# Stretches of 26 and 22 fill products, and written step orders, in a fused attention and token-MLP kernel

## The chip, the cores and the metric

One Trainium2 chip; the program runs on one of its cores. Its engines are TensorE (PE, with its weight loads shown apart as PEld), VectorE (DVE), ScalarE (ACT), GpSimd (POOL) and SyncE (SP, which issues the DMAs). The metric is the time of one execution in device microseconds; lower is better. A profile is one execution of the program as the hardware profiler saw it, and its times count from the first instruction.

## The reference

The input x has 2048 tokens of 640 channels. Two branches are computed from it and mixed by a gate per token.

```
g = sigmoid((x * gate_w).sum(-1, keepdims=True))
q = (x @ wq) in 32 heads of 20;  k = x @ wk;  v = x @ wv       # one k and one v of 20 for all heads
a = softmax(q k^T * 20**-0.5) v, heads side by side, @ wo
h = layernorm(x)                                                # per token
b = (gelu(h^T @ w1 + b1) @ w2 + b2)^T                           # over the tokens: 2048 -> 1728 -> 2048, per channel
out = g * a + (1 - g) * b
```

## The kernel before

Everything heavy is a matmul on TensorE, and the kernel uses the array in two halves of 64 rows. The contraction of a score (20 numbers, in a split of high and low parts, 60 or 62 rows) and that of an MLP product (64 rows at a time) each fill one half, so that two matmuls run side by side. A half is called a lane here.

**The steps.** Four kinds of work go to TensorE in the main loop:

- *F*, a fill product: one 64-row part of the MLP or of the output projection, 320 columns wide. In the first MLP product it stands at line 1069, in the second at 866, in the output projection at 1005. All fill products of one result add up in one PSUM bank, `g_bank`.
- *s*, a score tile (line 677): 128 keys by 512 queries into a PSUM bank of its own. ScalarE takes its exponential into a tile `p` (line 686), and the bank is free again.
- *m*, a tile for the row maxima of a later group of queries (line 508): 128 queries by 512 keys into a PSUM bank. VectorE reduces it to a maximum (line 514), and the bank is free again.
- *PV*, the product of the exponentials with v (line 788): all 128 rows of the array at once, into a bank that ScalarE copies to `part` (line 800) and GpSimd adds to a running sum (line 801).

Seven banks (three `ms`, three `s`, one `o`) go round among *s*, *m* and PV. `bank_take` and `bank_give` (475 to 484) decide while the program is written which bank a step gets: the one that a small clock of the planner expects to be free first. On the chip semaphores hold the step until that bank really is free.

**The loop.** It has 244 stretches, then a tail. In a stretch one lane (the X lane) runs scores and maxima, the other (the F lane) fill products and one or two *m* or *s*. Both lanes end in a PV of two key blocks; then the lanes change roles. Stretches 0 to 83 carry the first MLP product, 84 to 211 the second, 212 to 243 the output projection. The stretch numbers count from 0; stretch 0 stands ahead of the first PV.

One result of the first MLP product takes 96 fill products, 48 in each lane. `batches` (1078) cuts each lane's 48 into two, at 24, so that a result takes four stretches of 24. Of its 16 token blocks each has three fill products: high weights by high inputs, high weights by low inputs, low weights by high inputs. The weights come in quarters of four token blocks, that is 12 fill products in a lane: a DMA brings `wr`, GpSimd casts it to `wh` (133) and subtracts to `wl` (134). Per result the four quarters are called for by `w1_upto` at the ends of stretches of the result before.

**The order in a stretch.** `main` (1163) has for each length of a stretch a pattern: one string for the X lane, one for the F lane around its fill products.

```
    PATTERN = {24: ("msmsmmssmsmmsmss", "Fm"), 20: ("smsmssmmsmmssm", "mFs"), 21: ("smsmsmmssmmsmsm", "Fs"),
               15: ("smsmssmsmss", "mFs")}
```

So a stretch of 24 has 16 steps in the X lane and, in the F lane, 24 fill products and an *m*: 17 steps that take a bank, beside PV. How the two lanes are woven into the one instruction stream is a rule: at each turn the lane comes next that is free first by the planner's clock (an *s* or *m* takes 0.232 us there, an *F* 0.147 us), with a bank's expected release counted in for *s* and *m*. The lengths 20 and 21 belong to the second MLP product, 15 to the output projection.

Of the kernel before, what the change touches and what calls it, by code (L numbers as in the profile page):

```python
# [18 lines left out]
S, D, H, DH, F = 2048, 640, 32, 20, 1728  # L19
# [11 lines left out]
TAIL = 24  # L31
BLOCKS = (2, 3, 3, 4, 4, 4, 4)
NA = 8
SIXES = range(3)
LAST_M = 2
M_FIRST = 1
# [8 lines left out]
def mix_kernel(ctx: ExitStack, tc: tile.TileContext, A_x, A_wq, A_wk, A_wv, A_wo,  # L45
# [427 lines left out]
    USE = {"exp": ("act", 0.43, 0.477, 0.65), "max": ("dve", 0.43, 0.6, 0.735), "sum": ("dve", 0.35, 0.47, 0.6)}  # L473

    def bank_take():
        i = min(range(len(pool)), key=lambda j: pool[j][0])
# [193 lines left out]
    def qk(u, pr, b):  # L670
        n, kb = units[u]
        assert n in back_in
        if kb == 4 and pr == 0 and b == 0:
            new_q(n + 1)
        q = qtiles[n]
        s = lead_bank() if ps_l else bank_take()
        nc.tensor.matmul(s, kst[64 * b:64 * b + 62, kb * P:(kb + 1) * P], q[64 * b:64 * b + 62, pr, :],  # L677
                         start=True, stop=True)
        ready[u] = 0.0 if ps_l else max(ready.get(u, 0.0), bank_give(s, "exp"))
        p = next_p()  # L680
        ptiles[u, 2 * pr + b] = p

        behind, last["ins"] = last["ins"], None

        def exp():
            e = nc.scalar.activation(p, s, AF.Exp, scale=SCALE)  # L686
# [88 lines left out]
    otile, sums = [], [None]  # L775
    later = []

    def pv_group(us, keep=False):
        n, kb = units[us[0]]
        assert units[us[-1]][0] == n  # L780
        if not otile:
            otile.append(bank_take())
        o = otile[0]
# [5 lines left out]
                                 start=opened and i == 0, stop=(i == len(us) - 1) and (ends or not keep),  # L789
                                 skip_group_check=True)  # L790
        if not keep:
            begin = max(clock["act"], clock["pv"] + 0.14)
            clock["act"] = begin + 0.477
            pool.append((begin + 0.65, otile.pop()))
            if kb == 0:
                sums[0] = ev.tile([P, NB], F32, name="acc", bufs=2)
                nc.scalar.activation(sums[0], o, AF.Copy)
            else:
                part = ev.tile([P, NB], F32, name="part", bufs=2)
                nc.scalar.activation(part, o, AF.Copy)  # L800
                nc.gpsimd.tensor_add(sums[0], sums[0], part)  # L801
# [276 lines left out]
    def batches(tiles, counts):  # L1078
# [57 lines left out]
    AHEAD, DRAIN, ENTER, FIRST = 4, 0.19, 0.138, 0.1  # L1136
# [3 lines left out]
    def pattern(k):  # L1140
        return PATTERN[len(ph[k][0])]

    base = [[pattern(k)[int(k % 2 != h)].count("m") for k in range(len(ph))] for h in range(2)]

    def share(k):
        left = [32 * NU - x for x in given]
# [7 lines left out]
    lanes = [0.0, 0.0]  # L1154
    fresh = [True, True]

    def issue(b, us, f, t):
        clock["now"] = max(t, clock["now"])
        f()
        lanes[b] = clock["now"] + us + (FIRST if fresh[b] else 0.0)  # L1160
        fresh[b] = False

    def main(k, vs, n_max):
        b = k % 2
        fs, rest, done = ph[k]
        fs, done = list(fs), list(done)
        known, kept = set(row_max), set(sent)
        end = 2 * ((vs[-1] if vs else -1) + 1)
        xs, side = pattern(k)
        before, after = side.split("F")  # L1170
        need = end + AHEAD - sc[b]
        if xs.count("s") < need:
            i = len(xs) * 2 // 3
            xs = xs[:i] + "s" * (need - xs.count("s")) + xs[i:]
        while xs.count("s") > need:
            i = xs.rindex("s")
            xs = xs[:i] + xs[i + 1:]
        if xs.count("m") < n_max[b]:
            xs += "m" * (n_max[b] - xs.count("m"))
        while xs.count("m") > n_max[b]:  # L1180
            i = xs.rindex("m")
            xs = xs[:i] + xs[i + 1:]
        after += "m" * (n_max[1 - b] - (before + after).count("m"))
        while (before + after).count("m") > n_max[1 - b]:
            if "m" in after:
                after = after.replace("m", "", 1)
            else:
                before = before.replace("m", "", 1)
        before = "s" * (end - sc[1 - b] - (before + after).count("s")) + before
        xs, before, after = list(xs), list(before), list(after)  # L1190
        total, count = len(xs) + len(before) + len(after) + len(fs), 0
        while fs or after or before or xs:
            if count == (total + 1) // 2:
                settle()
            count += 1
            free = min(e for e, _ in pool)
            tx = max(lanes[b], free) if xs else 1e9
            tf = 1e9
            if before or (after and not fs):
                tf = max(lanes[1 - b], free)  # L1200
            elif fs:
                tf = lanes[1 - b]
            if len(xs) == 1 and fs and not after:
                tx = 1e9
            if tf < tx or tf == tx and not before:
                if before or not fs:
                    c = (before or after).pop(0)
                    issue(1 - b, X_US, (s_next if c == "s" else ms_next)(1 - b) or (lambda: None), tf)
                else:
                    issue(1 - b, F_US, fs.pop(0), tf)  # L1210
                    while done and not fs:
                        done.pop(0)()
            else:
                c = xs.pop(0)
                issue(b, X_US, (s_next if c == "s" else ms_next)(b) or (lambda: None), tx)
        ms_done()
        spare[0] = len(row_max) == NU
        settle(len(vs) == 2)
        if vs:
            n, kb = units[vs[0]][0] + 1, units[vs[0]][1]  # L1220
            if n in kept and n in qtiles and n not in back_in:
                fetch_max(n)
                back_in.add(n)
        for f in rest:
            f()
        for i in sorted(known - sent):
            store_max(i)
            sent.add(i)
        if vs:
            start = max([max(lanes) + DRAIN, min(e for e, _ in pool)] + [ready[v] for v in vs])  # L1230
            clock["pv"] = start + len(vs) * PV_US + ENTER
            lanes[:] = [clock["pv"]] * 2
            fresh[:] = [True, True]
            pv_group(vs)

    ps_l.clear()
# [6 lines left out]
    v = 0  # L1243
# [165 lines left out]
```

## Time and profile before

| | |
|---|---|
| runs | 1607.21, 1607.86 and 1607.96 us; median 1607.86 us |
| profiled execution, its span from the first to the last instruction | 1606.5 us |
| granted TensorE clock | 1.000 |
| busy: PE, DVE, ACT, POOL | 1600.9, 1355.0, 1309.1, 867.6 us |
| from the first PV (161.75 us) to the end of the first MLP product (656.26 us) | 494.51 us |
| second MLP product, to 1372.30 us | 716.04 us |
| output projection, to 1526.46 us | 154.16 us |
| tail, to 1606.5 us | 80.04 us |

The profiled execution's own time is its span; what the runs' median has beyond it (1.4 us) lies around the program. A PE that is busy all the time is not a PE at its peak here: a matmul counts as busy in one lane while the other lane may stand idle. So the busy shares do not say how much there is to gain, and the reading goes by single stretches: from one PV to the next, what is the last thing that PV waits for?

### The profile page before, as it was taken

To read this page: it belongs to the slowest core of one execution; us is meant where nothing else is said; L and a number is where in the kernel's file an instruction comes from. 1 tells how busy PE (TensorE), PEld (TensorE's weight loads), DVE (VectorE), ACT (ScalarE), POOL (GpSimd) and SP (SyncE) were. 2 spreads that over 40 slices of the span, in tenths; PEclk is the share of its full clock that TensorE was granted. 3 is DMA by queue.
4 is the path that set the end of the run, shared out by engine and by line. 5 is a ranking of instruction groups with operands and counts; after the bars stand their busy time and mean duration, and the time that the engine had idled before them with its cause. 6 is when DMAs were issued, how large, how long until landed. Compare 5 with 4: busy or idle time off the path is not lost.

```text
span 1606.5 us, 39460 instructions
## 1 busy us (share of the span) xinstructions
PE 1600.9 (100%) x14864; PEld 1123.2 (70%) x14864; DVE 1355.0 (84%) x2301; ACT 1309.1 (81%) x2566; POOL 867.6 (54%) x976
## 2 busy tenths in 40 slices
PE   9999999999999999999999999999999999999999
PEld 7899677767776777666666666666666666666676
DVE  6689999999999999888888888888888888766644
ACT  4546888888888888888888888888888888999974
POOL 6568676768777687644544434454544333344420
PEclk9999999999999999999999999999999999999999
DMA  7655223323233323222222122222222112245521
GB/s 218 212 171 143 73 74 80 86 64 94 76 81 85 82 67 80 64 73 81 73 70 68 51 67 67 70 73 81 73 73 69 54 50 68 85 123 181 165 87 57
DMA packets 183750, 145.07 MB, mean 90 GB/s; under 512 B 38291, under 2 KB 145424, under 8 KB 183560
## 3 DMA queue, kind: packets, MB, share of 16 engines
q1 hardware_dynamic: 183272, 142.23, 31.4%
q8 instruction: 117, 1.92, 0.5%
q14 instruction: 73, 0.60, 0.1%
q10 hardware_dynamic: 288, 0.33, 0.1%
HBM read 108.75 MB, written 32.15 MB: 88 GB/s over the span
## 4 chain that ended last, share of the span: by engine, by line
PE 98%; DVE 1%; POOL 0%; ACT 0%; issue 0%; DVEq 0%; POOLq 0%
PE s L788 16%; PE ms L788 11%; PE g L866 11%; PE s L677 10%; PE g L1069 9%; PE ms L677 9%; PE ms L508 6%; PE s L508 6%; PE pp L307 4%; PE o L677 3%; PE o L508 2%; PE g L1005 2%; PE o L788 2%; PE s L720 1%; PE g L720 1%; PE s L960 1%
## 5 line engine op out<-in xcount | busy, mean ns | idle before, releaser
L514 DVE TENSOR_REDUCE mp<-ms 128x1 f32<-128x512 f32 x889 | 583.1, 682 | 79.8 <-PE ms L508 64.9
L686 ACT ACTIVATE p<-s 128x512 f32<-128x512 f32 x938 | 543.2, 617 | 39.6 <-PE ms L788 12.8
L514 DVE TENSOR_REDUCE mp<-s 128x1 f32<-128x512 f32 x759 | 503.2, 683 | 75.1 <-PE s L508 61.0
L686 ACT ACTIVATE p<-ms 128x512 f32<-128x512 f32 x808 | 471.9, 614 | 35.1 <-PE s L788 11.8
L801 POOL TENSOR_TENSOR acc<-acc,part 128x512 f32<-128x512 f32 x213 | 275.0, 1291 | 311.2 <-ACT part L800 300.8
L677 PE MATMUL s<-qst,kst 62*128 62x512 f32 x944 | 362.9, 407 | 0.0
L508 PE MATMUL ms<-kst,qmx 60*128 60x512 f32 x889 | 357.5, 416 | 0.0
L677 PE MATMUL ms<-qst,kst 62*128 62x512 f32 x810 | 319.1, 407 | 0.0
L1069 PE MATMUL g<-slot,wh 64*128 64x320 f32 x1344 | 306.1, 313 | 0.3 <-ACT p L686 0.3
L508 PE MATMUL s<-kst,qmx 60*128 60x512 f32 x759 | 304.0, 414 | 0.2 <-DVE mp L514 0.2
L788 PE MATMUL s<-p,v_sb 128*32 128x512 f32 x2240 | 269.3, 598 | 0.0
L1069 PEld LDWEIGHTS g<-slot,wh 64*128 64x128 f32 x1344 | 216.6, 185 | 70.1 <-issue 49.4
L134 POOL TENSOR_TENSOR wl<-wr,wh 128x512 fp32r<-128x512 f32 (+1 forms) x176 | 218.1, 1239 | 28.0 <-ACT wh L131 16.3
L514 DVE TENSOR_REDUCE mp<-o 128x1 f32<-128x512 f32 x308 | 210.1, 682 | 18.5 <-PE o L508 17.8
L677 PEld LDWEIGHTS s<-qst,kst 62*128 62x128 f32 x944 | 174.2, 185 | 59.1 <-ACT p L686 27.6
L1069 PE MATMUL g<-slot,wl 64*128 64x320 f32 x672 | 205.4, 306 | 0.0
L866 PE MATMUL g<-u,wh 64*128 64x320 f32 x864 | 196.5, 309 | 0.0
L866 PE MATMUL g<-slot,wh 64*128 64x320 f32 x864 | 196.4, 309 | 0.0
L677 PEld LDWEIGHTS ms<-qst,kst 62*128 62x128 f32 x810 | 150.0, 186 | 56.8 <-ACT p L686 28.3
L788 PE MATMUL ms<-p,v_sb 128*32 128x512 f32 x1560 | 189.4, 598 | 0.0
L686 ACT ACTIVATE p<-o 128x512 f32<-128x512 f32 x273 | 168.3, 617 | 12.7 <-PE ms L788 6.9
L508 PEld LDWEIGHTS ms<-kst,qmx 60*128 60x128 f32 x889 | 164.2, 185 | 3.6
(270 smaller groups left out, 3101.8 us busy)
## 6 DMA issues: line engine op xcount, KB each, us to landing
wr<-in_B_w_dram SPq DMA_DIRECT2D x136, 256.0 KB
qmx<-q_scr SPq DMA_DIRECT2D x192, 80.0 KB
qst<-q_scr SPq DMA_DIRECT2D x192, 80.0 KB
ot<-l_scr SPq DMA_DIRECT2D x120, 64.0 KB
y_scr<-yo SPq DMA_DIRECT2D x16, 320.0 KB
slot<-o_scr SPq DMA_DIRECT2D x16, 320.0 KB
o_scr<-ot SPq DMA_DIRECT2D x124, 40.0 KB
o_scr<-acc SPq DMA_DIRECT2D x124, 40.0 KB
```

Of the source, the lines that this page charges most:

```text
L134: nc.gpsimd.tensor_sub(wl[:, :nv], wr[:, :nv], f32(wh[:, :nv]))
L307: nc.tensor.matmul(pp, w, t, start=first and n == 0, stop=not more and n == len(steps) - 1)
L508: nc.tensor.matmul(ms, qmax[n][64 * b:64 * b + 60, pr, qt * P:(qt + 1) * P], kst[64 * b:64 * b + 60, kq * NB:(kq + 1) * NB], start=True, s ...
L514: r = nc.vector.tensor_reduce(mtiles[n][:, c, kq:kq + 1], ms, axis=AX.X, op=ALU.max)
L677: nc.tensor.matmul(s, kst[64 * b:64 * b + 62, kb * P:(kb + 1) * P], q[64 * b:64 * b + 62, pr, :], start=True, stop=True)
L686: e = nc.scalar.activation(p, s, AF.Exp, scale=SCALE)
L720: nc.tensor.matmul(pu[r][:, :HD2], w[rows, c, :], h[rows, st, :], start=(st == 0 and k == 0), stop=(st == NS - 1 and k == 2))
L788: nc.tensor.matmul(o[32 * hh:32 * hh + 32, :], v_sb[:, kb + i, :], ptiles.pop((u, hh)), start=opened and i == 0, stop=(i == len(us) - 1) a ...
L801: nc.gpsimd.tensor_add(sums[0], sums[0], part)
L866: other_tile(half, nc.tensor.matmul(hold["p"][:, :HD2], w[r, i, :], u[d][r, fc, :], start=(hold["n"] == 1), stop=(hold["n"] == 6 * FC - 3)))
L1005: other_tile(half, nc.tensor.matmul(hold["p"][:, :HD2], o[r, c, :], w[r, c, d * HD2:(d + 1) * HD2], start=(hold["n"] == 1), stop=(hold["n" ...
L1069: other_tile(half, nc.tensor.matmul(hold["p"][:, :HD2], w[r, st % HS, :], h[d][r, st, :], start=(hold["n"] == 1), stop=(hold["n"] == 6 * NS)))
```

## The change

A result's 48 fill products of a lane are cut at 26, not at 24: two stretches of 26 fill products, one in each lane, then two of 22. The patterns and the rule that wove the lanes are gone. For each length a string gives the whole order of a stretch, both lanes in one; capital *M* and *S* are steps in the F lane. Where the number of steps does not fit (at the loop's ends), `fit` drops or adds some. The planner's clock, which still picks the banks, has new constants and a new notion of when a step starts (`issue`). A bank whose exponential must wait for the next PV, because all `p` tiles are taken, is kept out of the pool until that PV. In the tail, the blocks of PV from the fourth on call for the scores one step ahead per lane, not two.

```diff
+FIRST_F = 26
...
-    X_US, F_US, PV_US = 0.232, 0.147, 0.858
+    X_US, F_US, PV_US, LOAD = 0.2335, 0.147, 0.858, 0.1
...
+        if not ps_l and len(ptiles) >= len(ring):
+            late.append(pool.pop()[1])
...
+        while late:
+            pool.append((max(clock["now"], clock["act"]) + 2 * PV_US, late.pop()))
...
-                cut = [[len(r) * j // cnt for j in range(cnt + 1)] for r in rows]
+                cut = [[0, first, len(r)] if first else [len(r) * j // cnt for j in range(cnt + 1)] for r in rows]
...
-    seq = batches([b1_jobs(*t) for t in todo], [2] * len(todo))
+    seq = batches([b1_jobs(*t) for t in todo], [2] * len(todo), FIRST_F)
...
-    PATTERN = {24: ("msmsmmssmsmmsmss", "Fm"), 20: ("smsmssmmsmmssm", "mFs"), 21: ("smsmsmmssmmsmsm", "Fs"),
-               15: ("smsmssmsmss", "mFs")}
+    AHEAD, ENTER, EXIT = 4, 0.108, 0.135
+    ORDER = {26: "mFFsFmFsFFsFFmFmFsFFFsFmFFmFFsFFmFFmFFmFsMFs",
+             22: "sFmFFsFFFmsFFFmFssFFmFFFssFFFmmFFFsFmM",
+             20: "MsmFFsFsFsFFFFmFFsmFmFFFFmsFsFFsFFMm",
+             21: "MsFsFFmmFFsFFssFFFmsFFmFFFsmFFmFFsFFm",
+             15: "MsmFFsFFsFFmFsFFsFFmsFFFsFSm"}
...
+    def issue(h, us, f, free=0.0):
+        clock["issue"] = max(clock["issue"] + 0.004, begun[h], free)
+        begun[h] = clock["now"] = max(lanes[h], clock["issue"] + LOAD)
+        lanes[h] = begun[h] + us
+        f()
...
+            if c == "F":
+                issue(1 - b, F_US, fs.pop(0))
...
+                h = b if c in "sm" else 1 - b
+                step = (s_next if c in "sS" else ms_next)(h)
+                if step:
+                    issue(h, X_US, step, min(e for e, _ in pool))
...
-        ends = [min(2 * len(units), 2 * (v + n) + 2) for _ in range(2)]
+        ends = [min(2 * len(units), 2 * (v + n) + (2 if n < 3 else 1)) for _ in range(2)]
```

The changed program has the same matmuls as before, in other places. A stretch of 26 takes nine *m* and eight *s* in the X lane and one *M* in the F lane (18 steps with a bank), one of 22 seven *m*, eight *s* and one *M* (16); 20, 21 and 15 keep their numbers (16, 16 and 13).

The end of stretch 21, a stretch of the first MLP product, on TensorE as it was; `g` is the fill's bank, L677 a score, L508 a maxima tile, L788 the PV:

```order
L1069 MATMUL g<-slot_83,wh 128x320
L677 MATMUL s<-qst,kst 128x512
L1069 MATMUL g<-slot_83,wh 128x320
L1069 MATMUL g<-slot_83,wl 128x320
L508 MATMUL o<-kst,qmx 128x512
L1069 MATMUL g<-slot_83,wh 128x320 x2
L677 MATMUL ms<-qst,kst 128x512
L1069 MATMUL g<-slot_83,wl 128x320
L677 MATMUL ms<-qst,kst 128x512
L508 MATMUL ms<-kst,qmx 128x512
L788 MATMUL s<-p,v_sb 32x512 x8
```

The last maxima tile is the F lane's *m*, and it stands last of all. The same end in the changed program, where stretch 21 has 26 fill products (lines: L1074 fill, L678 score, L509 maxima, L793 PV), with the tiles' numbers:

```order
L509 MATMUL o_2334<-kst_71,qmx_3377 128x512
L1074 MATMUL g_1185<-slot0_83,wh_3955 128x320
L1074 MATMUL g_1185<-slot0_83,wl_3956 128x320
L509 MATMUL s_1186<-kst_71,qmx_3377 128x512
L1074 MATMUL g_1185<-slot0_83,wh_4141 128x320
L678 MATMUL ms_2331<-qst_3238,kst_71 128x512
L509 MATMUL s_1188<-kst_71,qmx_3377 128x512
L1074 MATMUL g_1185<-slot0_83,wh_4141 128x320
L678 MATMUL ms_2333<-qst_3238,kst_71 128x512
L793 MATMUL ms_2332<-p_4203,v_sb_72 32x512
```

The F lane's maxima tile now has a fill product and a score behind it, and the two fill products that came over from the later stretches read `wh_4141`, the cast of the weights' third quarter. Before, that quarter's first reader opened the third stretch of a result (stretch 22), as here:

```order
L1069 MATMUL g_1185<-slot0_83,wh_4141 128x320
L508 MATMUL s_1186<-kst_71,qmx_3367 128x512
L1069 MATMUL g_1185<-slot0_83,wh_4141 128x320
L677 MATMUL ms_2333<-qst_3234,kst_71 128x512
L1069 MATMUL g_1185<-slot0_83,wl_4142 128x320
```

In the changed program its first reader stands near the end of the result's first stretch (stretch 20), where the last three rows before PV are the same kinds of steps as in stretch 21 above.

More of the change, by code (lines that the diff above doesn't have):

```diff
@@ L773, in other_tile @@
         last["half"], last["ins"] = half, ins
-    otile, sums = [], [None]
+    otile, sums, late = [], [None], []
     later = []
@@ L791, in pv_group @@
         if not keep:
-            begin = max(clock["act"], clock["pv"] + 0.14)
+            begin = max(clock["act"], clock["pv"] + 0.336)
             clock["act"] = begin + 0.477
-            pool.append((begin + 0.65, otile.pop()))
+            pool.append((begin + 0.657, otile.pop()))
             if kb == 0:
@@ L1076, in b1_jobs, with batches @@
                         for st in range(NS) for k in range(3)], done)]
-    def batches(tiles, counts):
+    def batches(tiles, counts, first=None):
         out = []
@@ L1135, in mix_kernel, with order @@
     FREE_AT, ACT_AT = (0.3, 0.3, 0.3, 0.6, 1.3, 0.0, 0.3), 0.5
[L1136 to L1143 removed]
+    AHEAD, ENTER, EXIT = 4, 0.108, 0.135
[4 more added lines that the diff above has]
+             15: "MsmFFsFFsFFmFsFFsFFmsFFFsFSm"}
+    def order(k):
+        return ORDER[len(ph[k][0])]
+    base = [[order(k).count("m" if k % 2 == h else "M") for k in range(len(ph))] for h in range(2)]
     def share(k):
@@ L1152, in share, with fit @@
         return [c[k] - (i == h and k % 4 == 1 and k < m and over[h] > 0) for i, c in enumerate(base)]
[L1154 to L1158, printed above, removed]
-        f()
-        lanes[b] = clock["now"] + us + (FIRST if fresh[b] else 0.0)
-        fresh[b] = False
+    lanes, begun = [0.0, 0.0], [0.0, 0.0]
+    clock["issue"] = 0.0
+    def issue(h, us, f, free=0.0):
+        clock["issue"] = max(clock["issue"] + 0.004, begun[h], free)
+        begun[h] = clock["now"] = max(lanes[h], clock["issue"] + LOAD)
+        lanes[h] = begun[h] + us
+        f()
+    def fit(order, c, n):
+        while order.count(c) > n:
+            i = order.rindex(c)
+            order = order[:i] + order[i + 1:]
+        while order.count(c) < n:
+            i = order.rindex("F") * 2 // 3
+            order = order[:i] + c + order[i:]
+        return order
     def main(k, vs, n_max):
@@ L1168, in main @@
         end = 2 * ((vs[-1] if vs else -1) + 1)
[L1169 to L1186, printed above, removed]
-            else:
[L1188 to L1215, printed above, removed]
@@ new lines, in main @@
+        tokens = fit(order(k), "s", end + AHEAD - sc[b])
+        tokens = fit(fit(tokens, "m", n_max[b]), "M", n_max[1 - b])
+        tokens = "S" * (end - sc[1 - b]) + tokens
+        for i, c in enumerate(tokens):
+            if i == (len(tokens) + 1) // 2:
+                settle()
+            if c == "F":
+                issue(1 - b, F_US, fs.pop(0))
+                while done and not fs:
+                    done.pop(0)()
+            else:
+                h = b if c in "sm" else 1 - b
+                step = (s_next if c in "sS" else ms_next)(h)
+                if step:
+                    issue(h, X_US, step, min(e for e, _ in pool))
@@ L1216, in main @@
+        assert not fs and not done
         ms_done()
@@ L1229, in main @@
         if vs:
[L1230 to L1233, printed above, removed]
+            start = max([max(lanes) + ENTER, min(e for e, _ in pool)] + [ready[v] for v in vs])
+            clock["pv"] = start + len(vs) * PV_US
+            clock["issue"] = clock["pv"] + EXIT
+            lanes[:] = begun[:] = [clock["issue"]] * 2
             pv_group(vs)
```

2 lines of the change are left out of this document (1 added, 1 removed).

## The prediction

> **What bounds the kernel now.** The page first, its busy times; its chain of waits, too, runs on TensorE nearly all the way.
>
> ```profile
> PE 1600.9 (100%) x14864; PEld 1123.2 (70%) x14864; DVE 1355.0 (84%) x2301; ACT 1309.1 (81%) x2566; POOL 867.6 (54%) x976
> ```
>
> That hides the idle half of the array. So next come the stages, by the view of stretches of time restricted to the PV line (16 matmul records per PV):
>
> ```profile
> 161.75:656.26 494.51, 159.69 (x1329) 34.76 (x1329) 1.00 0.31 79
> 656.26:1372.30 716.04, 246.26 (x2048) 53.57 (x2048) 1.00 0.24 68
> ```
>
> The first MLP product has 1328/16 = 83 stretches of 494.51/83 = 5.958 us from PV to PV and the second 128 of 5.594. Now one stretch, 21, in the timeline of TensorE:
>
> ```profile
> 280.87 1.93 PE L788 MATMUL s<-p,v_sb 128*32 128x512 f32 x16
> 282.72 0.41 PE L1069 MATMUL g<-slot,wh 64*128 64x320 f32 x1
> 282.73 0.49 PE L508 MATMUL ms<-kst,qmx 60*128 60x512 f32 x1
> 282.97 0.30 PE L1069 MATMUL g<-slot,wh 64*128 64x320 f32 x1
> 283.06 0.39 PE L677 MATMUL ms<-qst,kst 62*128 62x512 f32 x1
> ...
> 285.47 0.45 PE L1069 MATMUL g<-slot,wh 64*128 64x320 f32 x2
> 285.65 0.39 PE L677 MATMUL s<-qst,kst 62*128 62x512 f32 x1
> ...
> 286.20 0.30 PE L1069 MATMUL g<-slot,wl 64*128 64x320 f32 x1
> ...
> 286.39 0.50 PE L508 MATMUL ms<-kst,qmx 60*128 60x512 f32 x1
> 286.82 0.64 PE L788 MATMUL s<-p,v_sb 128*32 128x512 f32 x4
> ```
>
> PV holds the array 282.72 - 280.87 = 1.85 us. Call 282.72 the stretch's zero. Fill products follow each other by (286.20 - 282.97)/22 = 0.147 us, steps of the X lane by (285.65 - 283.06)/11 = 0.235 us. The first of a lane takes 0.10 more: 0.25 to the second fill, 0.33 to the second step. The end:
>
> ```profile
> 286.39 0.18 PEld L508 LDWEIGHTS ms<-kst,qmx 60*128 60x128 f32 x1
> ```
>
> The F lane's last fill at 286.20 left that lane free at 286.35, yet the weights of its *m* load only at 286.39. A load that had to wait costs its lane 0.10 again, as at the start, so this *m* counts from 286.49; PV follows at 286.82, that is 0.235 for the *m* and some 0.095 to change over. The wait costs 286.49 - 286.35 = 0.14 us. What ended it is VectorE:
>
> ```profile
> 283.26 1.29 DVE L514 TENSOR_REDUCE mp<-ms 128x1 f32<-128x512 f32 x2 [0.36 <-PE ms L508]
> ...
> 285.66 0.68 DVE L514 TENSOR_REDUCE mp<-ms 128x1 f32<-128x512 f32 x1
> ```
>
> Two single reductions are left out between these rows, so the last row is the stretch's fifth; it ends at 285.66 + 0.68 = 286.34, and the load follows 0.05 later. VectorE came out of PV idle (0.36) and works without a gap from 0.54 on, a bank every 0.60: at 1.22, 1.82, 2.42, 3.02, 3.62. ScalarE's banks:
>
> ```profile
> 282.92 0.60 ACT L800 ACTIVATE part<-s 128x512 f32<-128x512 f32 x1 [1.17 <-PE s L788]
> 283.55 0.60 ACT L686 ACTIVATE p<-ms 128x512 f32<-128x512 f32 x1
> 284.04 1.22 ACT L686 ACTIVATE p<-s 128x512 f32<-128x512 f32 x2
> 285.16 1.08 ACT L686 ACTIVATE p<-ms 128x512 f32<-128x512 f32 x2
> 286.11 0.62 ACT L686 ACTIVATE p<-s 128x512 f32<-128x512 f32 x1
> ```
>
> The copy frees its bank at 0.80, exponentials at 1.43 and then about every 0.48 where a score is there (the pair at 285.16 takes 1.08, one alone 0.60). Up to 286.34 that is the copy, five exponentials and five reductions: eleven. Six banks were free at zero (seven less PV's); a step beyond the sixth waits for a release, the seventeenth for the eleventh. So **the bound is the seventeenth bank**, not a lane's work.
>
> **The first MLP product, worked out.** A step that gets its bank late can count from the release plus 0.05 plus 0.10.
>
> *26.* F lane: 0.10 + 26 x 0.147 + 0.235 = 4.157. X lane: 0.10 + 17 x 0.235 = 4.095. The order begins as before, *m* then *s*, so VectorE keeps its times. The scores stand earlier (second, fourth, fifth, eighth step), so ScalarE need not pause: 0.80, 1.43, 1.91, 2.39, 2.87, 3.35, 3.83. The eleventh release is still 3.62 and goes to the *M*, which counts from 3.77; its own place, behind 25 fills, is 0.10 + 25 x 0.147 = 3.775. Nothing is lost there. The twelfth, 3.83, goes to the last *s*: it counts from 3.98 against 3.86 and ends at 4.215. Without that wait the end is 4.157. I take 4.19, as ScalarE's clock moves by a few hundredths from stretch to stretch; PV to PV 4.19 + 0.095 + 1.85 = 6.135, between 6.10 and 6.16.
>
> *22.* F lane 0.10 + 22 x 0.147 + 0.235 = 3.57, X lane 0.10 + 15 x 0.235 = 3.625. The order begins with *s*, the first *m* is a step later, so VectorE's times are 0.235 later: 1.455, 2.055, 2.655, 3.255. ScalarE's, from a stretch of the second product that begins with a score (zero 753.55):
>
> ```profile
> 753.73 0.60 ACT L800 ACTIVATE part<-o 128x512 f32<-128x512 f32 x1 [0.30 <-PE o L788]
> 754.23 0.59 ACT L686 ACTIVATE p<-ms 128x512 f32<-128x512 f32 x1
> ...
> 756.13 0.65 ACT L686 ACTIVATE p<-s 128x512 f32<-128x512 f32 x1
> ```
>
> that is 0.78, 1.27 and every 0.48: 1.75, 2.23, 2.71, 3.19. Sixteen steps need the tenth release, 3.255; the last *M* counts from 3.405, ends at 3.64. PV to PV 3.65 + 0.095 + 1.85 = 5.595, between 5.57 (lanes alone) and 5.66 (a release 0.06 later).
>
> Mean (6.135 + 5.595)/2 = 5.865, against 5.958: 0.093 x 84 stretches = **7.8 us less**. The cut by itself gains nothing: the longer lane's mean is (4.157 + 3.625)/2 = 3.891 against 0.10 + 24 x 0.147 + 0.235 = 3.863 before. The gain is the 0.14 of waiting, less this 0.03 and the rests above. Bounds: lanes alone, 3.891 + 1.945 = 5.836, gains 10.2 us; the old 0.14 kept on both, 5.976, loses 1.5 us.
>
> **The rest.** A stretch of 20 keeps its 16 steps. Its end before (same stretch of the second product):
>
> ```profile
> 753.55 0.49 PE L677 MATMUL ms<-qst,kst 62*128 62x512 f32 x1
> 757.26 0.64 PE L788 MATMUL ms<-p,v_sb 128*32 128x512 f32 x4
> ```
> ```profile
> 756.83 0.18 PEld L677 LDWEIGHTS s<-qst,kst 62*128 62x128 f32 x1
> ```
>
> The last score loads 0.05 behind the exponential that ends at 756.78, the tenth release, and PV follows at 756.83 + 0.10 + 0.235 + 0.095. A new order asks for the tenth release too, and ScalarE cannot give it earlier: 0, for 96 stretches. Bounds: lanes alone, 0.10 + 20 x 0.147 + 2 x 0.235 = 3.51, would be 0.10 less each (9.6 us); 0.03 more each for another order's misfits is 2.9 us. A stretch of 21 waits for PV's own bank:
>
> ```profile
> 764.69 0.49 PE L677 MATMUL s<-qst,kst 62*128 62x512 f32 x1
> 768.47 1.92 PE L788 MATMUL ms<-p,v_sb 128*32 128x512 f32 x16
> ```
> ```profile
> 767.81 0.61 ACT L686 ACTIVATE p<-ms 128x512 f32<-128x512 f32 x1
> ```
>
> ScalarE frees it at 768.42, PV starts at 3.78. The new order puts an *M* and an *s* first, so the eleventh release is VectorE's 3.62, and the lanes decide: 0.10 + 15 x 0.235 + 0.095 = 3.72. That is 0 to 0.06 for 32 stretches; half of it is **1.0 us less**. The projection's 15 keep their 13 steps: 0, with 0.02 either way, 0.6 us. The tail's two deferred scores per block change places, not number: 0, within two steps, 0.5 us. Banks held out of the pool, and the new constants, only choose which bank; that is in the bounds.
>
> Sum: -7.8 - 1.0 = -8.8; I take 0.6 off for misfits of an order that cannot give way (below). Against the profiled 1606.5 that is 1598.3, against the runs' median 1607.86 - 8.2 = **1599.7 us**.
>
> **Rivals.** *More gain.* The orders let the second product's steps find their banks too: up to 7.8 + 32 x 0.06 + 9.6 = 19 us, 1588.5. For it: lanes alone would be that short. Against it: 16 steps and ten releases remain.
>
> *No gain: a fixed order holds what stands behind a late step.* Weight loads go out in program order:
>
> ```profile
> 767.97 0.18 PEld L677 LDWEIGHTS o<-qst,kst 62*128 62x128 f32 x1 [0.21 <-ACT p L686]
> 767.99 0.18 PEld L508 LDWEIGHTS ms<-kst,qmx 60*128 60x128 f32 x1
> ```
>
> The second load stood behind the first one's bank for as long. A fill has 0.147 - 0.10 = 0.047 us to spare for such a hold; beyond it the F lane, the long one in a 26, loses all. One hold of 0.10 per stretch of the first product takes 84 x 0.10 = 8.4 us: 1608. [...]
>
> *Slower: the third quarter's cast.* It must now be there in a result's first stretch. The nearest case (stretch 20):
>
> ```profile
> 276.77 0.41 PE L1069 MATMUL g<-slot,wh 64*128 64x320 f32 x1
> ```
> ```profile
> 276.99 1.30 POOL L839 TENSOR_TENSOR acc<-acc,ot 128x512 f32<-128x512 f32 x1 [4.07 <-DMA qmx<-q_scr]
> 279.57 0.61 POOL L133 CAST wh<-wr 128x512 fp32r<-128x512 f32 x1
> ```
>
> The cast ends at 280.18. The 25th fill counts from 276.77 + 3.63 = 280.40, so its load wants the cast by 280.25: 0.07 to spare, where a DMA held GpSimd back. That DMA chain falls on every second result, ten of 21. If GpSimd were later there by one accumulation (1.3 us), it would cost about 10 x 1.2 = 12 us: 1607.9 - 8.2 + 12 = 1612. It decides from 0.9 us on. Against it: the same DMAs, and a stretch 20 that grows by 0.18 gives them time.
>
> **How the numbers follow.** Forecast 0.77; more gain 0.06; holds 0.11; the cast 0.06. A run tells a change from about 0.2% (3.2 us). Faster: the forecast, more gain, and half of the holds: 0.77 + 0.06 + 0.05 = 0.88. Same: the other half and a third of the cast: 0.08. Slower: 0.04. The range: below, lanes alone in the first product (10.2) and 2 us from the 21s, -12; above, a hold of 0.05 in each of the 84 stretches (4.2 us) leaves -4. That is 1596 to 1604; what it leaves out is the most of the last three cases.
>
> **What would show it.** In the first product PV to PV alternates, two near 6.13 and two near 5.60; the last *s* of a 26 and the last *M* of a 22 load 0.05 behind a release, and the *M* of a 26 no longer. The second product stays at 5.57 for 20 and comes to about 5.60 for 21. TensorE waits for POOL nowhere in the loop. The prediction is wrong if 26 and 22 add up to more than 11.85, if fills stand behind steps that wait, or if the second product moves by more than 3 us.

## The result: slower, and the profile after

| | before | changed |
|---|---|---|
| runs, median (lowest to highest) | 1607.91 us (1607.21 to 1608.23) | 1633.73 us (1631.04 to 1636.75) |
| ratio, with its 95% interval | | 1.0162 (1.0148 to 1.0176) |
| span of the profiled execution | 1606.5 us | 1635.0 us |

The changed kernel is 1.6% slower, where 0.5% faster was predicted. The profiled execution is the longest of its four runs (1636.75 us), so the stages below differ by a little more than the medians do. The page of the changed kernel: first its busy times, then its chain of waits by engine, then one of its costliest groups (busy us, mean ns of one, then the idle time ahead of them and what ended it).

```profile
PE 1605.3 (98%) x14864; PEld 1125.4 (69%) x14864; DVE 1361.1 (83%) x2301; ACT 1286.6 (79%) x2566; POOL 868.0 (53%) x976
...
PE 89%; DMA 5%; POOL 2%; SPq 1%; DVE 1%; issue 1%; ACT 0%; POOLq 0%; DVEq 0%
...
L871 PE MATMUL g<-u,wh 64*128 64x320 f32 x864 | 200.3, 311 | 23.9 <-POOL wh L134 23.9
```

Before, PE was busy all the time and 98% of the chain. Now 5% of the chain is DMA and 2% GpSimd, and the second MLP product's fills (L871, which was L866) stand idle 23.9 us for GpSimd's cast of the weights (L134, which was L133). The stages, by the view of stretches of time restricted to the PV line (L793, which was L788): first MLP product, second, projection, tail from its first PV to its last.

```profile
161.89:650.51 488.62, 159.68 (x1329) 34.64 (x1329) 1.00 0.31 80
650.51:1399.23 748.72, 253.33 (x2049) 54.03 (x2049) 0.99 0.23 65
1399.23:1554.37 155.14, 61.56 (x513) 13.36 (x513) 1.00 0.46 137
1554.37:1620.96 66.59, 20.33 (x176) 4.99 (x176) 1.00 0.24 72
```

The first product, which the change was made in, went from 494.51 to 488.62 us: 5.9 us less. The second went from 716.04 to 748.72 us: 32.7 us more, and there alone the granted clock is under 1. Projection and tail took 1.0 and 0.6 us more (154.16 and 66.04 before).

The 32.7 us sit in a few stretches. The median stretch of the second product is 5.57 us from PV to PV in both kernels. But in the changed kernel, from stretch 92 to 204 every eighth one takes 6.1 to 8.3 us (15 of them, 26.5 us over 5.57 in all), and six times the stretch behind such a one takes about 7.1 us (9.3 us over in all). 26.5 + 9.3 = 35.8, and what is left over, -3.1, is the rest of the stage, which became shorter. The view of waits of TensorE in that stage has one row alone (us in total, times, longest); in the first product it has none.

```profile
PE g L871 <- POOL wh L134: 23.9, 15, 2.6
```

**Where the wait comes from.** One of these stretches is 132, around 937 us. In the timeline of TensorE:

```profile
936.78 0.31 PE L871 MATMUL g<-u,wh 64*128 64x320 f32 x1
938.74 0.41 PE L871 MATMUL g<-u,wh 64*128 64x320 f32 x1 [1.62 <-POOL wh L134]
```

GpSimd at that time, in the changed kernel:

```profile
936.28 1.28 POOL L844 TENSOR_TENSOR acc<-acc,ot 128x512 f32<-128x512 f32 x1 [5.82 <-DMA qst<-m_scr]
...
938.17 0.51 POOL L134 CAST wh<-wr 128x384 fp32r<-128x384 f32 x1
```

The cast that the fill needs ends at 938.68. It stands behind the *scale* of a finished result (L844, the product with the reciprocals of its sums), and the scale had waited 5.82 us for a DMA. For the same result before, the wait is 0.39 us:

```profile
924.00 1.28 POOL L839 TENSOR_TENSOR acc<-acc,ot 128x512 f32<-128x512 f32 x1 [0.39 <-DMA ot<-l_scr]
...
925.90 0.51 POOL L133 CAST wh<-wr 128x384 fp32r<-128x384 f32 x1
```

The scale needs `ot`, into which four DMAs broadcast the reciprocals, and these follow the store of the reciprocals (`l_scr<-rl`). SP's queue in the kernel before, around that result (start, time that SP spends on issuing, DMA):

```profile
909.48 2.20 SPq L147 DMA_DIRECT2D qst<-q_scr  x6
916.07 0.35 SPq L831 DMA_DIRECT2D l_scr<-rl  x1
916.46 0.57 SPq L567 DMA_DIRECT2D qst<-m_scr  x2
917.08 2.08 SPq L115 DMA_DIRECT2D wr<-in_B_w_dram  x2
919.26 2.85 SPq L835 DMA_DIRECT2D ot<-l_scr  x4
...
922.89 2.33 SPq L147 DMA_DIRECT2D qmx<-q_scr  x6
```

And in the changed kernel:

```profile
922.97 0.35 SPq L836 DMA_DIRECT2D l_scr<-rl  x1
923.68 2.37 SPq L116 DMA_DIRECT2D wr<-in_B_w_dram  x2
926.10 2.33 SPq L148 DMA_DIRECT2D qmx<-q_scr  x6
928.47 3.92 SPq L148 DMA_DIRECT2D qst<-q_scr  x6
932.43 1.70 SPq L840 DMA_DIRECT2D ot<-l_scr  x4
```

From the store to the broadcast it was 919.26 - 916.07 = 3.19 us; now it is 932.43 - 922.97 = 9.46. Two groups of six loads of the next result's q (`qst` for the scores, `qmx` for the maxima), 2.33 + 3.92 = 6.25 us of SP's time, have come to stand ahead of the broadcast. The first used to go out ahead of the store, the second behind the broadcast. (GpSimd's row names another DMA, `qst<-m_scr`, as the end of its wait; that is the one that landed last by the profile, and SP issues it right behind the broadcast. The scale itself reads `acc` and `ot`. It starts 936.28 - 934.13 = 2.15 us after SP has issued the last of the four broadcasts, 924.00 - 922.11 = 1.89 before.)

Why they moved is in the code. The loads are no step of their own; a score and a maximum call them on the way:

```
def qk(u, pr, b):
    n, kb = units[u]
    if kb == 4 and pr == 0 and b == 0:
        new_q(n + 1)
```

The six `qst` loads go out where lane 0's first score of quarter 4 is written, the six `qmx` loads where the slower lane reaches its first maximum of the next result (`min(issued) == 32 * n + 1`). The pattern of a stretch of 20 or 21 had an *s* in the F lane as well, so lane 0's score came in stretch 8n+1, ahead of the store; the written orders of 20 and 21 have no *S*, so it comes one stretch later, between store and broadcast. The maxima's place moved the other way.

### The profile page after: what moved, and what is told of

Its sections match the earlier page's. It is cut to its first block, busy times and chain, and to the rows that moved or that the text cites. A ratio compares the mean times of both kernels' runs of the same rounds, so it can differ in the third digit from the quotient of the medians.

```text
span 1635.0 us, 39447 instructions
## 1 busy us (share of the span) xinstructions
PE 1605.3 (98%) x14864; PEld 1125.4 (69%) x14864; DVE 1361.1 (83%) x2301; ACT 1286.6 (79%) x2566; POOL 868.0 (53%) x976
## 4 chain that ended last, share of the span: by engine, by line
PE 89%; DMA 5%; POOL 2%; SPq 1%; DVE 1%; issue 1%; ACT 0%; POOLq 0%; DVEq 0%
PE s L793 14%; PE ms L793 11%; PE g L871 9%; PE ms L509 8%; PE s L509 7%; PE g L1074 7%; PE s L678 6%; PE ms L678 6%; PE pp L308 4%; PE o L509 3%; PE s L723 2%; PE o L793 2%; DMA qst<-q_scr 2%; PE g L1010 2%; PE o L678 2%; SPq L148 1%
## 5 line engine op out<-in xcount | busy, mean ns | idle before, releaser
L515 DVE TENSOR_REDUCE mp<-ms 128x1 f32<-128x512 f32 x860 | 564.9, 682 | 86.1 <-PE ms L509 30.1
L515 DVE TENSOR_REDUCE mp<-s 128x1 f32<-128x512 f32 x784 | 517.9, 682 | 73.3 <-PE o L678 20.7
L689 ACT ACTIVATE p<-s 128x512 f32<-128x512 f32 x901 | 530.8, 632 | 5.1 <-PE s L678 2.6
L689 ACT ACTIVATE p<-ms 128x512 f32<-128x512 f32 x855 | 505.9, 631 | 12.5 <-PE ms L678 5.3
L678 PE MATMUL s<-qst,kst 62*128 62x512 f32 x903 | 347.2, 406 | 0.0
L509 PE MATMUL ms<-kst,qmx 60*128 60x512 f32 x860 | 331.0, 411 | 0.0
L678 PE MATMUL ms<-qst,kst 62*128 62x512 f32 x861 | 330.7, 408 | 0.0
L1074 PE MATMUL g<-slot,wh 64*128 64x320 f32 x1344 | 308.6, 309 | 0.0
L509 PE MATMUL s<-kst,qmx 60*128 60x512 f32 x784 | 304.0, 411 | 0.5 <-DVE mp L515 0.5
L793 PE MATMUL s<-p,v_sb 128*32 128x512 f32 x2008 | 249.3, 611 | 0.0
L871 PE MATMUL g<-u,wh 64*128 64x320 f32 x864 | 200.3, 311 | 23.9 <-POOL wh L134 23.9
L1074 PEld LDWEIGHTS g<-slot,wh 64*128 64x128 f32 x1344 | 222.4, 184 | 0.0
L1074 PE MATMUL g<-slot,wl 64*128 64x320 f32 x672 | 212.4, 316 | 0.0
L793 PE MATMUL ms<-p,v_sb 128*32 128x512 f32 x1728 | 208.8, 601 | 0.1
L509 PEld LDWEIGHTS ms<-kst,qmx 60*128 60x128 f32 x860 | 155.6, 185 | 75.9 <-ACT p L689 27.9
L871 PE MATMUL g<-slot,wh 64*128 64x320 f32 x864 | 195.3, 308 | 0.0
L509 PEld LDWEIGHTS s<-kst,qmx 60*128 60x128 f32 x784 | 142.8, 185 | 67.6 <-ACT p L689 27.1
L678 PEld LDWEIGHTS s<-qst,kst 62*128 62x128 f32 x903 | 167.1, 186 | 20.6 <-DVE mp L515 15.9
L678 PEld LDWEIGHTS ms<-qst,kst 62*128 62x128 f32 x861 | 158.7, 186 | 21.0 <-DVE mp L515 15.9
```

The source lines that it names most:

```text
L509: nc.tensor.matmul(ms, qmax[n][64 * b:64 * b + 60, pr, qt * P:(qt + 1) * P], kst[64 * b:64 * b + 60, kq * NB:(kq + 1) * NB], start=True, s ...
L515: r = nc.vector.tensor_reduce(mtiles[n][:, c, kq:kq + 1], ms, axis=AX.X, op=ALU.max)
L793: nc.tensor.matmul(o[32 * hh:32 * hh + 32, :], v_sb[:, kb + i, :], ptiles.pop((u, hh)), start=opened and i == 0, stop=(i == len(us) - 1) a ...
L871: other_tile(half, nc.tensor.matmul(hold["p"][:, :HD2], w[r, i, :], u[d][r, fc, :], start=(hold["n"] == 1), stop=(hold["n"] == 6 * FC - 3)))
L1074: other_tile(half, nc.tensor.matmul(hold["p"][:, :HD2], w[r, st % HS, :], h[d][r, st, :], start=(hold["n"] == 1), stop=(hold["n"] == 6 * NS)))
```

## The experiments

The theory (Q, for the queue): SP issues one DMA behind the other (in the changed kernel's rows above the last three groups start 0.04 or 0.05 us behind the end of the one ahead); twelve loads ahead of the broadcast make it 6.3 us late; GpSimd's scale waits; the cast stands behind the scale, the fills wait for the cast. Its rivals: O, the written orders themselves make something late, wherever the loads stand; C, the clock falls for another reason and the stalls follow.

**One line in the changed kernel puts the six `qst` loads back ahead of the store.**

```diff
-        if kb == 4 and pr == 0 and b == 0:
+        if kb == 4 and pr == 0 and b == 1:
             new_q(n + 1)
```

> The changed kernel, with one edit: the six loads of the next result's q (new_q) are called by lane 1's score of quarter 4 instead of lane 0's, a stretch earlier; the written orders stay. In the second MLP product they then stand in SP's queue ahead of the reciprocals' store (l_scr<-rl), as they did before the change; the other six loads (qmx) still stand ahead of the broadcast of the reciprocals (ot). Theory Q (SP's queue: the twelve moved loads delay the broadcast, GpSimd's scale waits for it, the cast of W2 stands behind the scale, the fills wait for the cast): the broadcast comes 3.9 us earlier, more than the stalls of about 1.75 us; the long stretches at every eighth place go, the second product takes 713 to 716 us instead of 748.7, no halved clock, the whole 1600 to 1603 us. Theory O (the written orders of 20 and 21 themselves make steps or casts late, wherever the loads stand): the second product stays near 748 us and the whole above 1628. Theory C (the clock is halved for another reason, the stalls follow): the six pieces of 3.41 us at half clock stay, about 10 us, 1610 to 1612.

Measured: 1600.55 us (1600.18 to 1600.80), ratio to before 0.9952 (0.9937 to 0.9967). First and second product, SP's queue and GpSimd's scale at the same result:

```profile
161.35:649.89 488.54, 159.66 (x1328) 34.64 (x1329) 1.00 0.31 80
649.89:1362.71 712.82, 246.25 (x2049) 53.42 (x2049) 1.00 0.24 68
```
```profile
908.41 0.35 SPq L836 DMA_DIRECT2D l_scr<-rl  x1
...
911.58 2.28 SPq L148 DMA_DIRECT2D qmx<-q_scr  x6
913.91 3.03 SPq L840 DMA_DIRECT2D ot<-l_scr  x4
```
```profile
918.79 1.28 POOL L844 TENSOR_TENSOR acc<-acc,ot 128x512 f32<-128x512 f32 x1 [2.92 <-DMA ot<-l_scr]
```

The broadcast stands 5.50 us behind the store. The scale still waits 2.92 us, but TensorE no longer waits for GpSimd, and the whole loss is gone: 1633.73 to 1600.55 us with the orders untouched. That is against O. The clock is full again in the second product (1.00), which is against C; so is the changed kernel's own trace, where only six of the fifteen stalls have a slow stretch behind them.

**The other half: hold back the six `qmx` loads.**

```diff
             if min(issued) == 32 * n + 1:
-                new_qmax(n + 1)
+                if any(f and f.__name__ in ("inverse", "inverse_in") for _, f in later):
+                    held_q.append(n + 1)
+                else:
+                    new_qmax(n + 1)
...
             def inverse_in():
                 ...
+                while held_q:
+                    new_qmax(held_q.pop(0))
```

> The changed kernel, with one edit: the other six loads (qmx, new_qmax) are held back while a reciprocal's store or broadcast is still to come, and issued right behind the broadcast; the six loads of q stay ahead of it. Theory Q: the broadcast comes about 2.3 us earlier, by itself more than the 1.75 us of a typical stall but less than the longest (2.6): the second product 714 to 722 us, the whole 1601 to 1609 us. Theory O: above 1628.

Measured: 1600.92 us, ratio 0.9954 (0.9939 to 0.9969), second product 712.83 us: better than expected, for the broadcast came 5.5 us behind the store (4 us earlier than in the changed kernel, not 2.3; the `qst` loads took 2.33 us of SP's time here, not 3.92). So neither group is harmful alone; it takes both. There is a cover (a time by which the broadcast can be late at no cost), and it is shorter than the two together.

**GpSimd's order instead of SP's.** Here SP keeps the late broadcast, and the scale, with the two steps that follow it, moves behind the casts.

```diff
-            first = ... (sums_out, sums_in, None, inverse, inverse_in, None, scale)
+            first = ... (sums_out, sums_in, None, inverse, inverse_in, None, None, None, scale)
```

> The changed kernel, with GpSimd's scale (and the two steps behind it) two places later in the list of deferred work, so that the casts of W2 stand ahead of it in GpSimd's order; SP's queue keeps the changed order and the broadcast is as late as in the changed kernel. Theory Q: GpSimd's wait for the broadcast then holds no cast; the stalls of the second product go (713 to 718 us), the whole 1600 to 1606. If instead the late thing is the load of the weights itself in SP's queue, or the orders, the fills still wait for the cast: above 1625. The results of the heads are written two places later, which could cost a wait of its own where the buffers of acc and ot come round, up to a few us.

Measured: 1601.03 us, ratio 0.9955 (0.9939 to 0.9972), second product 712.89 us. SP's queue and GpSimd around the same result:

```profile
908.46 0.34 SPq L836 DMA_DIRECT2D l_scr<-rl  x1
...
917.55 1.70 SPq L840 DMA_DIRECT2D ot<-l_scr  x4
```
```profile
915.89 0.50 POOL L134 CAST wh<-wr 128x384 fp32r<-128x384 f32 x1
...
921.40 1.29 POOL L844 TENSOR_TENSOR acc<-acc,ot 128x512 f32<-128x512 f32 x1
```

The broadcast is as late as in the changed kernel (9.09 us behind the store) and costs nothing, as the cast now goes ahead of the scale. This shows the middle link: the late DMA matters only because GpSimd's scale waits for it with the cast behind it. No cost of the later results showed.

**The other direction: extra loads in the kernel before.** Twelve small loads of q into a tile that nobody reads, ahead of the broadcast, for the results whose broadcasts fall in the second product.

```diff
             def inverse_in():
+                if 10 <= n <= 24:
+                    for i in range(12):
+                        ...
+                        nc.sync.dma_start(out=idle[o:o + DH, :, c * 64:(c + 1) * 64], in_=...)
                 for hh in range(4):
```

> The kernel before, its orders untouched, with twelve extra small loads of q into a tile that nobody reads (10 KB each), ahead of the broadcast of the reciprocals, for the results 10 to 24, those of the second MLP product; they add work that the reference has no need of. Theory Q: the broadcast comes 4.5 to 6.2 us later there, GpSimd's scale and the cast behind it too; stretches at every eighth place grow by 1 to 2.6 us, some with a halved clock behind them; the second product grows from 716 by 15 to 40 us, the whole is 1622 to 1648. Theory O: the place of loads in SP's queue does not matter, the whole stays within 0.3% of 1608.

Measured: 1613.56 us (1611.43 to 1614.67), ratio 1.0032 (1.0020 to 1.0044): slower, but by 5.3 us instead of 14 to 40. That is at the edge of the 0.3% that O allowed, so the time alone does not rule O out. The trace does: fills wait for GpSimd's cast four times in the second product, 2.8 us in all, where the kernel before has no such wait.

```profile
161.23:655.83 494.60, 159.67 (x1329) 34.63 (x1329) 1.00 0.31 79
655.83:1378.18 722.35, 246.23 (x2049) 53.42 (x2049) 1.00 0.25 70
```
```profile
918.04 0.35 SPq L832 DMA_DIRECT2D l_scr<-rl  x1
...
926.29 1.71 SPq L843 DMA_DIRECT2D ot<-l_scr  x4
```
```profile
930.32 1.30 POOL L847 TENSOR_TENSOR acc<-acc,ot 128x512 f32<-128x512 f32 x1 [4.55 <-DMA m_scr<-mt]
```

The scale starts 930.32 - 918.04 = 12.28 us behind the store, against 924.00 - 916.07 = 7.93 before and 936.28 - 922.97 = 13.31 in the changed kernel. The expectation had left out the cover. If the cover is what the theory says, four more loads must cost far more than the twelve did:

> The kernel before with sixteen extra loads of q ahead of each broadcast in the second MLP product, where twelve made GpSimd's scale 4.35 us later and cost 6.3 us in all. Four more take 4 x 0.42 = 1.7 us of SP's queue, so the scale is 6.0 us late. Theory Q (the lateness beyond a cover of about 4 us comes out one for one at every eighth stretch): the sixteen long stretches, 0.41 us on the mean with twelve loads, grow by 1.0 to 1.7 each, the second product is 738 to 752 us, the whole 1624 to 1638, the clock halved behind the stalls that leave TensorE idle for the most of one 3.41 us piece. If the loads cost something else (DMA traffic that slows the others), four more cost a third more of what twelve did: second product near 724, the whole near 1615.6.

Measured, with sixteen loads: 1638.79 us (1635.91 to 1641.38), ratio 1.0193 (1.0177 to 1.0208), a little above the top of the range. The second product:

```profile
655.69:1405.50 749.81, 252.80 (x2049) 54.14 (x2049) 0.99 0.24 68
```

That is the changed kernel's loss, made in the kernel before, with its own rule for the orders: 749.81 us against 748.72, the granted clock 0.99 in both. The loads themselves cost little (716.04 to 722.35 us with twelve); what counts here is when the scale starts behind the store. Over the fourteen results whose scale falls in the stretches 92 to 196 of the second product (91 to 195 in the kernel before):

| kernel | broadcast behind store, us | scale behind store, us | second product, us |
|---|---|---|---|
| before | 3.2 to 3.5 | 7.5 to 9.0 | 716.04 |
| `qst` loads ahead of the store | 5.5 | 9.2 to 11.4 | 712.82 |
| before, twelve loads | 7.8 to 9.1 | 11.1 to 12.8 | 722.35 |
| changed | 8.1 to 9.5 | 12.7 to 14.3 | 748.72 |
| before, sixteen loads | 9.3 to 10.7 | 12.6 to 14.5 | 749.81 |
| changed, scale behind the casts | 7.8 to 9.6 | 12.9 to 14.4 | 712.89 |

The results with the stretches they make longer, in the changed kernel: 13.44 us and 1.90 over 5.57 (stretch 92), 13.31 and 1.79 (132), 12.67 and 1.18 (148), 14.14 and 2.60 (164); with twelve loads 12.78 and 1.21 (92), 12.28 and 0.55 (132). The difference is 11.5 to 11.7 each time, 11.3 to 11.8 over all fifteen long stretches of the changed kernel, 11.2 to 11.6 with sixteen loads, and with twelve 11.5 to 11.7 in six and 10.9 in one (stretch 140). So the cover is about 11.5 us from the store to the scale, in the old orders and the new, and each microsecond beyond it comes out one for one. It is the cover of the cast, not of the scale: in the last row the scale is beyond 11.5 us for every result and nothing is lost, as the cast no longer stands behind it.

**The `qst` loads alone moved in the kernel before.**

```diff
-        if kb == 4 and pr == 0 and b == 0:
+        if kb == 4 and pr == 1 and b == 0:
             new_q(n + 1)
```

> The kernel before, its rule for the orders untouched; only the six loads of the next result's q are called by the score of the second pair of heads (pr 1) of lane 0 in quarter 4 instead of the first, so they stand between the reciprocals' store and their broadcast in the second MLP product and in the projection. Theory Q: the broadcast is 2 to 4 us later, within the cover of about 4 us that the runs with twelve loads showed; the second product 716 to 719 us, the whole within 3 us of before. If the place ahead of the broadcast itself is harmful, whatever the time: over 1620.

Measured: 1608.07 us, ratio 1.0002 (0.9992 to 1.0012), the second product 716.02 us. The broadcast is 5.5 to 5.7 us behind the store, the scale 9.8 to 11.4: inside the cover, and no cost, as expected.

**The cut without the queue.** The last run asks what the first product's gain is due to. It has the written orders and the loads in their old place, but the cut 24 and 24.

```diff
-FIRST_F = 26
+FIRST_F = 24
...
+             24: "mFFsFmFsFFsFFmFmFsFFFsFmFFmFFsFFmFFmFsMFs",
```

> The changed kernel with lane 1 calling the loads of q, and with the first MLP product cut 24 and 24 again, its order written out too: the 26's order less two fills, the M ahead of the last s. Theory B (the seventeenth bank bounds a stretch of 24, whoever sets the order; only the cut takes the wait away): the last s waits for the eleventh release at 3.62, counts from 3.77, ends at 4.005; PV to PV 5.95, the first product stays at 493 to 496 us, the whole 1606 to 1608. Theory W (it is the written order that gains, the cut only moves work): F lane 0.10 + 24 x 0.147 + 0.235 = 3.86, PV to PV 5.81 to 5.86, the first product 482 to 487 us, the whole 1595 to 1600.

Measured: 1606.04 us (1605.42 to 1606.60), ratio 0.9988 (0.9979 to 0.9997). First and second product:

```profile
161.75:655.61 493.86, 159.68 (x1329) 34.65 (x1329) 1.00 0.30 80
655.61:1368.56 712.95, 246.23 (x2049) 53.42 (x2049) 1.00 0.24 68
```

493.86/83 = 5.95 us per stretch, as the rule gave it (5.958). Its stretch 22 (zero at 288.56) still ends on the eleventh release, VectorE's at 292.18, 3.62 after zero; the last score loads 0.05 behind it:

```profile
290.90 1.28 DVE L515 TENSOR_REDUCE mp<-ms 128x1 f32<-128x512 f32 x2
...
292.23 0.18 PEld L678 LDWEIGHTS ms<-qst,kst 62*128 62x128 f32 x1
```

So this written order, which keeps *s* early, does not help a stretch of 24; with the orders of 26 and 22 the cut took 493.86 - 488.54 = 5.3 us off the first product. The second product's 3.1 us of gain belong to the orders of 20 and 21.

## Why the prediction was wrong, step by step

**The step that failed** stands under "The rest": "A stretch of 20 keeps its 16 steps", and so 0 for 96 stretches. It counted banks and lanes of the second product, and they do stay: the ordinary stretch is 5.57 us as before. It did not count that two of the moved steps call loads, six DMAs each, and past which DMAs of SP's queue these moved. The prediction looked at the order of TensorE, VectorE and ScalarE alone. Twelve loads, 6.25 us of SP's time against 2.5 to 4.0 us of spare time (11.5 less the 7.5 to 9.0 from store to scale before), cost 35.9 us between the second product with them (748.72) and without (712.82).

**The rival of the late cast** had the right mechanism, a DMA that holds GpSimd with the cast behind it, and was given 0.06. It was placed in the first product, where the cast of the third quarter is needed earlier; there TensorE waited for GpSimd nowhere. Its price, ten results by 1.2 us, was a third of what 15 results in the second product cost. "Against it: the same DMAs" was the error in the reasoning: the DMAs are the same, their order is not.

**The first product** was right in mechanism and nearly in size: -5.9 us instead of -7.8. The stretches of 22 take 5.59 and 5.60 us (medians of the two lanes' stretches), predicted 5.595. Stretch 42 begins with the PV at 403.73, so its zero is at 405.58. VectorE's last release and the load of the last *M*:

```profile
407.56 1.28 DVE L515 TENSOR_REDUCE mp<-ms 128x1 f32<-128x512 f32 x2
...
408.89 0.18 PEld L509 LDWEIGHTS ms<-kst,qmx 60*128 60x128 f32 x1
```

The pair of reductions ends at 408.84, 3.26 after zero, where 3.255 was worked out; the load follows 0.05 later and PV 0.43 after it, at 409.32. The stretches of 26 take 6.15 and 6.21 us, predicted 6.135. In stretch 40 (zero 393.21):

```profile
396.39 0.64 ACT L689 ACTIVATE p<-ms 128x512 f32<-128x512 f32 x1
...
397.09 0.18 PEld L678 LDWEIGHTS ms<-qst,kst 62*128 62x128 f32 x1
397.52 0.16 PEld L793 LDWEIGHTS s<-p,v_sb 128*32 128x32 f32 x8 [0.25 <-DVE mp L515]
```

The last *s* loads behind the exponential that ends at 397.03, 3.82 after zero: the twelfth release, worked out as 3.83. The prediction then took 4.19 for the end between 4.157 without the wait and 4.215 with it; the wait is always there. In the second 26 of each result ScalarE is another 0.06 later (stretch 41: its first exponential begins 0.83 us after zero, not 0.77), so the twelfth release is at 3.88. That is the mis-sized term: (6.148 + 6.206)/2 - 6.135 = 0.042 on 42 stretches, 1.8 us. Why ScalarE begins later there I did not test. "The *M* of a 26 no longer" loads behind a release was wrong by a hair: it does (396.89, behind a reduction that ends at 396.83), and counts from 3.77, its own place, so nothing is lost.

**The second product without the stalls** gains 3.2 us (712.82 with the loads put back), predicted 1.0. The 32 stretches of 21 come from a mean of 5.655 to 5.586 us, 0.07 each and 2.2 us in all, where half of up to 0.06 was taken; the 96 of 20 lose 0.01 each, 1.0 us. **Projection and tail** lose 0.98 and 0.55 us where 0 within 0.6 and 0 within 0.5 were given; with the loads put back they lose 0.94 and 0.54, so it is the new orders there, and which step does it stays open. **Holds** did not show in the first product, whose sizes leave no room for 0.10 per stretch, and **more gain** did not either. The pair of weight loads shown for the holds is not a clear case, as a reduction of VectorE ended at 767.93, 0.06 us ahead of the second load. A clearer one is in stretch 21 before: the load of a maxima tile starts at 285.80, 0.06 us behind the end of a reduction (285.74), and the fill's load that stands behind it in the program starts at 285.80, too, 0.19 us behind the fill's load ahead of it (285.61) and not 0.147.

With the loads in their old place the kernel gains 7.7 us (1600.55 against 1608.22), close to the 8.2 of the sum. That closeness is partly luck: about 2 us less than forecast in the first product and 2 us more in the second cancel, and of the 1.5 us lost behind them 0.6 had been taken off in the sum for another reason. The prediction said that it would be wrong if the second product moved by more than 3 us, and that TensorE would wait for POOL nowhere in the loop; both fell.

## What to carry to other kernels

Where the order of compute steps is written anew, list for each DMA queue what stands between a DMA that somebody waits for and the DMA ahead of it, before and after; a load that a step calls on the way moves with the step. Then follow the wait to its end: here GpSimd passed a late DMA on to the cast behind its scale, which has nothing to do with the transfer (fills waited 23.9 us for the casts in the changed kernel, and nowhere in the second product with the scale behind them). And look for the cover by adding cheap loads in two amounts: the first twelve cost 5 us, the next four 25.

## What the runs showed of the hardware that was not expected

Behind six of the fifteen stalls of the changed kernel the next stretch was slow, too: 6.96 to 7.19 us, where the median is 5.57. The view of stretches of time for TensorE there, cut into pieces of 3.41 us (length, PE busy, granted clock, DMA share, GB/s):

```profile
699.87:703.28 3.41, 1.66 (x16) 1.00 0.47 151
703.28:706.69 3.41, 3.41 (x19) 0.50 0.35 106
747.66:751.07 3.41, 1.74 (x17) 1.00 0.50 159
751.07:754.48 3.41, 3.41 (x18) 0.50 0.34 106
935.39:938.80 3.41, 1.79 (x22) 1.00 0.48 156
938.80:942.21 3.41, 3.41 (x30) 1.00 0.33 102
```

The granted clock was 0.50 for 3.41 us six times (from 703.28, 751.07, 798.86, 1078.75, 1126.54 and 1222.11) and 1.00 in the pieces right ahead and behind. The six begin at distances that are multiples of one length: 751.07 - 703.28 = 47.79 = 14 x 3.413, and so for all. In the 3.41 us ahead of the six, TensorE was busy for 0.96 to 1.74 us; in the least busy piece around each of the other stalls from stretch 116 to 196, cut at the same distances, for 1.79 to 2.38, and no halved one followed. In the kernel with sixteen loads, 1.80 was followed by a halved one (896.64 to 900.05, clock 0.50), and the stall from 1223.29 to 1225.86, in which TensorE stood idle for 2.11 us, by none. It is split over two of the pieces:

```profile
1220.90:1224.31 3.41, 2.85 (x30) 1.00 0.40 112
1224.31:1227.72 3.41, 1.86 (x14) 1.00 0.72 217
1227.72:1231.14 3.42, 3.42 (x39) 1.00 0.49 154
```

So the length of a stall does not decide by itself in these runs: 1.75 us of idle time, up to 701.95 in the changed kernel, was followed by a halved clock, and these 2.11 us were not. That TensorE must be idle for the most of one piece, as the expectation for the sixteen loads had it, was the author's estimate; no run shows what sets off a halving. Each halved piece cost about 1.55 us more in the changed kernel (9.3 us in six).

One halving lasted longer, in the kernel with sixteen loads: its maxima and score matmuls, 0.39 or 0.40 us long ahead of the stall, took 0.62 us each at 945.06 and still at 950.64, and the PV between them 3.64 us, where PV takes 1.93 in stretch 21 before. TensorE was busy for 3.20 us of the first halved piece, and the cause of the second stays open:

```profile
944.42:947.83 3.41, 3.20 (x14) 0.50 0.70 218
```

SP's time per load was not fixed either: over the second product, six `qst` loads took it 2.20 to 3.59 us in the kernel before and, right behind six others, 2.34 to 3.92 us in the changed kernel. SP's time for twelve such loads, 6.25 us at the result above, was what the loss came from. No run moved the loads to another engine.
